# Linear attention and two expanding layers: weights converted in 512-column pieces in their own places, and 124 due times set one by one

## The chip, the cores and the metric

The kernel runs on one core of a Trainium2 chip. The metric is the device time of one execution in microseconds (us); a run's time is the median of its executions. Five engines work side by side, each on its own list of instructions in order: TensorE (PE in the rows; its weight loads are PEld), VectorE (DVE), ScalarE (ACT), GpSimd (POOL) and SyncE (SP), which here only issues transfers between the main memory and the on-chip memory.

## The reference

```python
def phi(x):                                   # x: q or k, [4, 8, 576, 64]
    proj = np.einsum('bhsd,df->bhsf', x, w_phi)            # 64 -> 128 features
    proj = proj - np.max(np.abs(proj), axis=-1, keepdims=True)
    return np.concatenate([np.exp(proj), np.exp(-proj)], axis=-1)
kv = einsum('bhsf,bhsd->bhfd', phi(k), v);  z = phi(k).sum(2)
x  = einsum('bhsf,bhfd->bhsd', phi(q), kv) / (einsum('bhsf,bhf->bhs', phi(q), z) + 1e-06)
x  = x.transpose(0, 2, 1, 3).reshape(2304, 512)
h = x @ w_in1;  x = where(h > 0, h, exp(min(h, 0)) - 1) @ w_out1     # 512 -> 2048 -> 512
h = x @ w_in2;  x = (h * cos(h)) @ w_out2                           # 512 -> 2048 -> 512
```

q, k, v and w_phi are float32. [...]

## The kernel before, in words

**Attention.** For each of the four batches, `keys` takes five tiles of 128 rows (the last has 64). Each tile is loaded (k, and v beside it), projected on PE in two halves, each half gets its largest magnitude and the difference on DVE (`shifted`), two exponentials on ACT, and a product with v on PE (`times_v`). For batch 0 the sums over the rows are a PE product with ones in the same step (L458); for the others DVE adds the exponentials up (L480). `sums` then copies and transposes the result. `queries` and `results` do the same for 18 tiles of q: projection, difference, transposes, exponentials, product (L571), reciprocal, result into `xy`.

**The two layers.** `block` goes over columns of `xy` (the token rows), `step` over 16 groups j of 128 hidden units. A step has a first product (`g1`, L710), the nonlinearity on ACT and DVE, and a second product (`g2`, L718). Each factor is split into a rounded high and a low part, and each product is three passes. Layer 1 runs in two parts: j = 0 to 7 in nine blocks of 256 columns, laid among the attention, then j = 8 to 15 in six of 384 columns. Then layer 2 in six blocks of 384 columns.

**The weights.** `convert` makes a high and a low float32 part of each float64 piece of 256 columns: the load from SP into one of four buffers `raw` (L350), two scalings on ACT (L353, L356), a shift and a joining on DVE (L360, L364), an addition on POOL (L368), the high part on ACT (L379), the low part on POOL (L382). A load waits until its `raw` buffer has been read, so the four buffers also hold the loads back.

**What sets the order.** Every piece of work is a task with an engine, an estimated duration and a due time. `plan` takes the tasks in time order on its own estimates: among those that can begin, the one with the earliest due time, in the place (a buffer or a bank) that comes free first. It counts 0.7 for the SP part of a weight load and a fixed delay until it has landed; how many bytes are under way it doesn't count. The order it finds is then written out on each engine, and there every engine works strictly in that order. Where the plan sees PE idle in the first 70 us, `keep_busy` puts matmuls of no use (`spare`, L826) in.

**Transfers.** All loads but the first two small ones are issued on SP, in one queue. In the program's order each transfer waits for the eighth before it to have landed (the semaphores DMAHW0 to DMAHW7 in the rows of order below), beside the wait for its place.

Of the kernel before, what the change touches and what calls it, by code (L numbers as in the profile page):

```python
# [8 lines left out]
F32 = mybir.dt.float32  # L9
# [20 lines left out]
CH = 256  # L30
NC = NK * P // CH
# [39 lines left out]
NL, W1LATE, NEQ, EARLY = 4, -24.05, 4, 176.41  # L71
# [4 lines left out]
ND, NKF, NVT, NQF, RAWB, NE = 5, 2, 2, 2, 4, 5  # L76
# [15 lines left out]
class Task:  # L92


    def __init__(self, engine, cost, due, fn, writes=(), reads=(), after=(), latency=None, port=False):
# [9 lines left out]
        self.bufs = [b for b in dict.fromkeys(list(writes) + list(reads)) if isinstance(b, Buf)]  # L105
# [114 lines left out]
def body(tc, qt, kt, vt, wphi, w1, w2, out):  # L220
# [81 lines left out]
    AP, AK, AQ = ("a0", "a1"), ("a2", "a3"), ("a0", "a1", "a2", "a3")  # L302

# [18 lines left out]
    LOWS = [("wa", f"l{i}") for i in range(2 * NC * JA + NL)]  # L322

    def columns(b, k):

        at = k * P % CH
        return b.tile[:, at:at + P]

    def convert(pool, m, j, due, pace=1.0, after=()):

        for io in range(2):
            for c in range(NC):
                h = [(pool, f"h{j}_{io}_{c}")]
                l = LOWS if pool == "wa" else [(pool, f"l{j}_{io}_{c}")]
                whole = Buf(LOWS, [P, CH])  # L340
                W[m, j, io, c] = Buf(h, [P, CH], F32R), Buf(l, [P, CH], F32R)
                convert_piece(whole, Buf(h, [P, CH], I32), m, j, io, c, due, after)
                split(whole, m, j, io, c, due)
                due += pace

    def convert_piece(f, r, m, j, io, c, due, after):
        raw = buf("stg", "raw", RAWB, [P, CH, 2], U32)

        def load():
            nc.sync.dma_start(raw.tile, ws[m][j, :, io, c * CH:(c + 1) * CH])  # L350

        def scale():
            nc.scalar.activation(f.tile, raw.tile[:, :, 1].bitcast(F32), AF.Copy, scale=2.0 ** -112)  # L353

        def rest():
            nc.scalar.activation(r.tile, raw.tile[:, :, 0], AF.Copy, scale=2.0 ** -29)  # L356

        def shift():
            e = f.tile.bitcast(U32)
            nc.vector.tensor_scalar(e, e, 3, None, ALU.logical_shift_left)  # L360

        def join():
            e = f.tile.bitcast(U32)
            nc.vector.scalar_tensor_tensor(e, raw.tile[:, :, 1], 0x80000000, e, ALU.bitwise_and, ALU.bitwise_or)  # L364

        def add():
            e = f.tile.bitcast(I32)
            nc.gpsimd.tensor_tensor(e, e, r.tile, ALU.add)  # L368

        task("SP", 0.7, due - 20, load, [raw], [f, r], after, latency=2.2)  # L370
        task("ACT", cost(ACT_, CH), due, scale, [f], [raw])
        task("ACT", cost(ACT_, CH), due, rest, [r], [raw])
        task("DVE", cost(DVE1, CH), due, shift, [f], port=True)
        task("DVE", cost(DVE_, CH), due, join, [f], [raw], port=True)
        task("POOL", cost(POOL_, CH), due, add, [f], [r])

    def split(f, m, j, io, c, due):
        h, l = W[m, j, io, c]
        task("ACT", cost(ACT_, CH), due, lambda: nc.scalar.copy(h.tile, f.tile), [h], [f])  # L379
# [43 lines left out]
    def keys(b, due, pace, after=()):  # L423
# [4 lines left out]
        for t in range(5):  # L428
            r, du = ST[t], due + t * pace
            kf, v = buf("at", "kf", NKF, [P, 4, P]), buf("at", "vt", NVT, [P, H, D])  # L430
            ds = [buf("at", "d", ND, [P, 4, NF]) for _ in range(2)]

            def load(kf=kf, t=t, r=r):
                nc.sync.dma_start(kf.tile[:, :, 0:r], kt[b, :, :, t * P:t * P + r])
# [4 lines left out]
            task("SP", 0.85, du - (20 if b else KLOAD), load, [kf], [], after, latency=2.2)  # L439
# [85 lines left out]
    def queries(T, due, pace):  # L525

        q = buf("at", "qf", NQF, [P, 4, P])
# [164 lines left out]
    def step(m, j, i, last, xs, xb, ys, yp, hs, N, due, pace, late):  # L692
        wi, wo = ([b for c in range(NC) for b in W[m, j, io, c]] for io in range(2))
# [30 lines left out]
        in_line("g1", task("PE", 12 * mr_cost(N), d1, g1, [hp], [*wi, *xb], line["g1"]))  # L724
# [46 lines left out]
        task("PE", 12 * mr_cost(N), d2, g2, ys, [sh, *wo])  # L771
# [118 lines left out]
```

## Time and profile before

| what | value |
|---|---|
| median of 3 runs | 997.42 us (996.88 to 998.33) |
| the profiled execution | 997.03 us |
| its span, first to last instruction | 995.2 us |
| PE busy | 982.6 us, 99% |
| DVE, ACT, POOL busy | 716.5, 504.3, 209.6 us |
| moved by transfers | 63.28 MB |

PE is busy for 99% of the span, but some of that is `spare` matmuls of no use, and all of the waiting is in the first tenth and behind the last product. So a change can only pay in the first 100 us, and it can lose anywhere. The stretch is to be read by engine and by the transfers, not by the averages over the span.

### The profile page before, as it was taken

The numbers are of one execution on the slowest core, as the hardware profiler recorded it, in microseconds if no ns is written. First come the engines' busy times: TensorE is split into PE (matmuls) and PEld (weight loads), VectorE is DVE, ScalarE is ACT, GpSimd is POOL, SyncE is SP. The second block draws the span as 40 slices with busy tenths as digits, with TensorE's granted clock in tenths as the row PEclk, the third lists the DMA queues.
The fourth block names the chain that finished last, engine by engine and source line by source line (L and its number), as shares of the span: only waits on it lengthen the run. The fifth ranks groups of instructions, "written<-read, shape, count | busy, mean of one in ns | idle before, by whom it ended". The sixth has DMA issues, their size and how long they took to land.

```text
span 995.2 us, 21100 instructions
## 1 busy us (share of the span) xinstructions
PE 982.6 (99%) x8422; PEld 944.5 (95%) x8422; DVE 716.5 (72%) x1423; ACT 504.3 (51%) x1196; POOL 209.6 (21%) x262
## 2 busy tenths in 40 slices
PE   8998999999999999999999999999999999999998
PEld 6787988988899999999999999999999999999998
DVE  6999978778676678988344679975666666756664
ACT  6886754545546768876322576742232332423322
POOL 3556300000002546674000265600000000000000
PEclk9999999999999999999999999999999999999999
DMA  7544212120103344442012232100000000000000
GB/s 235 174 125 141 87 49 81 34 69 19 46 12 97 96 127 144 154 149 75 1 33 74 75 106 77 63 33 1 1 33 1 1 33 1 32 1 1 32 1 32
DMA packets 45889, 63.28 MB, mean 64 GB/s; under 512 B 5728, under 2 KB 24800, under 8 KB 45792
## 3 DMA queue, kind: packets, MB, share of 16 engines
q1 hardware_dynamic: 45632, 61.88, 19.6%
q8 instruction: 66, 1.08, 0.5%
q14 instruction: 31, 0.25, 0.1%
q10 hardware_dynamic: 160, 0.07, 0.0%
HBM read 52.49 MB, written 9.44 MB: 62 GB/s over the span
## 4 chain that ended last, share of the span: by engine, by line
PE 90%; DVE 4%; ACT 2%; issue 1%; POOL 1%; DMA 1%; DVEq 0%
PE y L718 24%; PE h L710 23%; PE a L710 15%; PE a L718 15%; PE a L571 4%; PE a L399 3%; PE a L451 3%; PE a L548 1%; POOL l L368 1%; DVE m L412 1%; DVE l L364 1%; DVE ek L480 1%; DVE d L415 1%; DVE l L360 1%; PE y L458 1%
## 5 line engine op out<-in xcount | busy, mean ns | idle before, releaser
L710 PE MATMUL h<-x,h 128*128 128x256 f32 (+1 forms) x1152 | 253.0, 309 | 0.1
L718 PE MATMUL y<-s,h 128*128 128x256 f32 (+1 forms) x956 | 202.7, 304 | 0.4 <-DVE s L767 0.4
L710 PEld LDWEIGHTS h<-x,h 128*128 128x128 f32 x1152 | 191.6, 188 | 5.1 <-issue 3.3
L710 PE MATMUL h<-x,l 128*128 128x256 f32 (+1 forms) x576 | 176.6, 307 | 1.4 <-POOL l L382 1.4
L368 POOL TENSOR_TENSOR l<-l,h 128x256 int32<-128x256 int32 x128 | 105.9, 834 | 301.7 <-DMA raw<-w 189.8
L718 PEld LDWEIGHTS y<-s,h 128*128 128x128 f32 x956 | 156.2, 188 | 4.0 <-issue 1.9
L710 PE MATMUL a<-x,h 128*128 128x384 f32 x576 | 146.1, 334 | 0.0
L718 PE MATMUL y<-s,l 128*128 128x256 f32 (+1 forms) x478 | 143.8, 301 | 0.0
L382 POOL TENSOR_TENSOR l<-l,h 128x256 fp32r<-128x256 f32 x128 | 105.4, 832 | 132.2 <-ACT h L379 131.2
L710 PEld LDWEIGHTS h<-x,l 128*128 128x128 f32 x576 | 108.2, 188 | 1.6 <-POOL l L382 1.6
L752 ACT ACTIVATE gq<-gq,pihalf 128x384 f32<-128x384 f32 x96 | 59.2, 617 | 97.9 <-DVE gq L749 97.8
L710 PEld LDWEIGHTS a<-x,h 128*128 128x128 f32 x576 | 103.9, 188 | 0.0
L718 PE MATMUL a<-s,h 128*128 128x384 f32 x380 | 96.4, 334 | 0.0
L710 PE MATMUL a<-x,l 128*128 128x384 f32 x288 | 96.2, 334 | 0.0
L718 PEld LDWEIGHTS y<-s,l 128*128 128x128 f32 x478 | 89.8, 188 | 0.0
L379 ACT CAST h<-l 128x256 fp32r<-128x256 f32 x128 | 51.7, 406 | 42.6 <-POOL l L368 41.7
L364 DVE SCALAR_TENSOR_TENSOR l<-raw,l 128x256 uint32<-128x256 uint32 x128 | 68.7, 550 | 1.1
L718 PEld LDWEIGHTS a<-s,h 128*128 128x128 f32 x380 | 68.6, 188 | 0.0
L718 PE MATMUL a<-s,l 128*128 128x384 f32 x190 | 63.5, 334 | 0.0
L353 ACT ACTIVATE l<-raw 128x256 f32<-128x256 f32 x128 | 55.9, 437 | 10.1 <-DMA raw<-w 10.0
L767 DVE TENSOR_TENSOR s<-gq,s 128x384 fp32r<-128x384 f32 x95 | 58.6, 616 | 3.2 <-ACT s L263 0.8
L360 DVE TENSOR_SCALAR l<-l 128x256 uint32<-128x256 uint32 x128 | 51.3, 416 | 11.5 <-ACT l L353 9.5
(111 smaller groups left out, 1667.5 us busy)
## 6 DMA issues: line engine op xcount, KB each, us to landing
raw<-w SPq DMA_DIRECT2D x128, 256.0 KB, 3.0
qf<-qt SPq DMA_DIRECT2D x18, 256.0 KB, 2.7
part<-o SPq DMA_DIRECT2D x18, 256.0 KB, 2.4
oq<-part SPq DMA_DIRECT2D x12, 384.0 KB, 3.4
out<-oq SPq DMA_DIRECT2D x12, 384.0 KB, 2.5
kf<-kt SPq DMA_DIRECT2D x16, 256.0 KB, 3.5
vt<-vt SPq DMA_DIRECT2D x16, 256.0 KB, 2.9
kf<-kt SPq DMA_DIRECT2D x4, 128.0 KB, 3.5
```

The costliest lines, as they stand in the source:

```text
L353: nc.scalar.activation(f.tile, raw.tile[:, :, 1].bitcast(F32), AF.Copy, scale=2.0 ** -112)
L360: nc.vector.tensor_scalar(e, e, 3, None, ALU.logical_shift_left)
L364: nc.vector.scalar_tensor_tensor(e, raw.tile[:, :, 1], 0x80000000, e, ALU.bitwise_and, ALU.bitwise_or)
L368: nc.gpsimd.tensor_tensor(e, e, r.tile, ALU.add)
L379: task("ACT", cost(ACT_, CH), due, lambda: nc.scalar.copy(h.tile, f.tile), [h], [f])
L382: nc.gpsimd.tensor_sub(l.tile, f.tile, h.tile.bitcast(F32))
L399: nc.tensor.matmul(pp[odd].tile[0:r, i * NF:(i + 1) * NF], x.tile[rows, i, 0:r], ww[rows], start=(i == 0), stop=True, skip_group_check=True,)
L571: nc.tensor.matmul(ns[odd].tile[32 * h:32 * h + 32, g * P + lo:g * P + hi], k[:, half, h // 2, at:at + 32] if g < 2 else k[:, half, 2, 32 ...
L710: nc.tensor.matmul(hp.tile[:, 0:N], columns(W[m, j, 0, kk * P // CH][a], kk), xs[kk][c](), start=(kk == 0 and n == 0), stop=(kk == NK - 1 ...
L718: nc.tensor.matmul(yp(dt), columns(W[m, j, 1, dt * P // CH][a], dt), (hi, lo)[c](), start=(i == 0 and n == 0 and (late or dt % 2 == 0)), s ...
L752: nc.scalar.activation(g.tile[:, 0:N], g.tile[:, 0:N], AF.Sin, bias=pihalf)
L767: nc.vector.tensor_sub(lo(), g.tile[:, 0:N], hi().bitcast(F32))
```

## The change

A weight piece is now 512 columns (half as many instructions, each twice as wide). Its raw numbers land where the high and low part will lie in the end, so that no `raw` buffers are left and a load of layer 1 waits for no buffer. The work in between is in three buffers `f` of two halves. Key and query tiles share four places `xf` in place of two `kf` and two `qf`. The key tile 2 of batch 0 is loaded from ACT's queue. The first four query tiles may use the banks h0, h1 and y0 too. And `MOVED` sets the due time of 124 tasks, by their number, and for some the engine.

```diff
-ND, NKF, NVT, NQF, RAWB, NE = 5, 2, 2, 2, 4, 5
+ND, NXF, NVT, NE = 5, 4, 2, 5
+NF_, RLEAD = 3, 20.0
+TEX, ONACT = 4, 3
+MOVED = {
+    2: -47, 10: 623, 14: 538, 26: 86, 36: 242, 46: 65, 52: -99, 53: -27, 54: -0, 58: -35, 66: 122, 68: -96,
...
+        moved = MOVED.get(len(tasks), t.due)
+        t.due, only = moved if isinstance(moved, tuple) else (moved, None)
+        t.choice = {only: t.choice[only]} if only else t.choice
...
+    AE = (*AQ, "h0", "h1", "y0")
...
-        raw = buf("stg", "raw", RAWB, [P, CH, 2], U32)
+    def convert_piece(place, m, j, io, due, after):
+        raw, w = Buf(place, [P, WD, 2], U32), Buf(place, [P, 2 * WD], F32R)
+        f = buf("stg", "f", NF_, [P, 2, WD])
+        W[m, j, io] = w
...
-            nc.sync.dma_start(raw.tile, ws[m][j, :, io, c * CH:(c + 1) * CH])
+            nc.sync.dma_start(raw.tile, ws[m][j, :, io])
...
-        task("SP", 0.7, due - 20, load, [raw], [f, r], after, latency=2.2)
+        task("SP", 0.7, due - RLEAD, load, [raw], [], after, latency=3.4)
...
+        task("ACT", cost(ACT_, WD), due, high, [w], [f])
+        task("POOL", cost(POOL_, WD), due, low, [w], [f])
...
-            kf, v = buf("at", "kf", NKF, [P, 4, P]), buf("at", "vt", NVT, [P, H, D])
+            kf, v = buf("at", "xf", NXF, [P, 4, P]), buf("at", "vt", NVT, [P, H, D])
...
+            side = b == 0 and 2 <= t < ONACT
+            queue = nc.scalar if side else nc.sync
...
-        shifted(q, due, P, ds, () if T < QFREE else done, (*AQ, "h0", "h1") if T < 2 else AQ)
+        shifted(q, due, P, ds, () if T < QFREE else done, (*AQ, "h0", "h1") if T < 2 else AQ if T >= TEX else AE)
...
+        ax = AE if T < TEX else AQ
+        tts, ns = [bank(*ax) for _ in range(2)], [bank(*ax) for _ in range(2)]
```

On SP, the loads that stand around the v tile of key tile 2 in batch 0 (vt0_58) in the kernel before; raw is a weight piece, kf a key tile, qf a query tile, and the brackets hold what each waits for:

```order
L350 DMA raw0_48_258<-w1 128x512 [waits DMAHW6_49,DVE_49,Activation_49]
L350 DMA raw1_53_268<-w1 128x512 [waits DMAHW7_49,DVE_49,Activation_49]
L434 DMA kf0_57_293<-kt 128x4x64 [waits DMAHW2_49,DMAHW0_49,PE_49]
L437 DMA vt0_58_302<-vt 128x512 [waits DMAHW1_49,PE_49]
L350 DMA raw2_66_324<-w1 128x512 [waits DVE_49,Activation_49]
L350 DMA raw3_70_333<-w1 128x512 [waits DMAHW3_49,DVE_49,Activation_49]
L437 DMA vt1_78_353<-vt 128x512 [waits DMAHW4_49,PE_49]
```

The same place now (vt0_50 is that v tile, w2_0 the first half of the weights of j = 2, xf2_45 a query tile):

```order
L364 DMA w2_0_31_203<-w1 128x1024 [waits DMAHW6_49]
L364 DMA w2_1_34_210<-w1 128x1024 [waits DMAHW7_49]
L364 DMA w3_0_39_234<-w1 128x1024 [waits DMAHW0_49]
L364 DMA w4_1_41_240<-w1 128x1024 [waits DMAHW1_49]
L364 DMA w5_0_44_247<-w1 128x1024 [waits DMAHW2_49]
L546 DMA xf2_45_252<-qt 128x512 [waits DMAHW3_49,PE_49]
L364 DMA w5_1_48_275<-w1 128x1024 [waits DMAHW4_49]
L364 DMA w6_0_49_280<-w1 128x1024 [waits DMAHW5_49]
L453 DMA vt0_50_283<-vt 128x512 [waits DMAHW6_49,PE_49]
L364 DMA w6_1_57_303<-w1 128x1024 [waits DMAHW7_49]
L364 DMA w7_0_58_307<-w1 128x1024 [waits DMAHW0_49]
L364 DMA w7_1_64_325<-w1 128x1024 [waits DMAHW1_49]
```

Of weights, six pieces of 256 columns stand ahead of that v tile on SP before, and eleven of 512 columns now; they no longer wait for DVE and ACT. In all, 18 weight pieces of 512 columns stand ahead of the v tile of key tile 4 (vt0_89).

On PE, the end of batch 0's keys and the first transposes of a query tile (L548) before, with vt0_98 the v tile of key tile 4:

```order
L399 MATMUL a_107_461<-ww,qf_33_188 128x128
L451 MATMUL a_40_225<-ek_95_414,vt_98_439 64x256 x4
L451 MATMUL a_41_226<-ek_97_436,vt_98_439 64x256 x4
L458 MATMUL y_42_227<-ek_95_414,ones 32x256 x4
L458 MATMUL y_42_227<-ek_97_436,ones 32x256 x4
L548 MATMUL a_123_521<-ident,d_93_402 128x128 x4
L548 MATMUL a_124_522<-ident,d_94_403 128x128 x4
```

And now:

```order
L412 MATMUL a_92_432<-ww,xf_71_358 128x128
L565 MATMUL h_95_444<-ident,d_78_374 128x128 x4
L565 MATMUL h_96_445<-ident,d_79_375 128x128 x4
L467 MATMUL a_35_212<-ek_82_390,vt_89_420 64x256 x4
L467 MATMUL a_36_213<-ek_87_416,vt_89_420 64x256 x4
L474 MATMUL y_37_214<-ek_82_390,ones 32x256 x4
L474 MATMUL y_37_214<-ek_87_416,ones 32x256 x4
```

The transposes went ahead of the last product with v, into the banks h0 and h1. The rest of batch 0's keys stands on PE as before. Of `spare` matmuls there are 25 in place of 35, 10 in place of 12 of them ahead of key tile 2.

On POOL, the additions and low parts of weights for j = 9 to 12 before (l3, l26, l28 are places of the work in between):

```order
L368 TENSOR_TENSOR l28_901_4966<-l28_901_4966,h9_1_1_902_4967 128x256
L382 TENSOR_TENSOR l9_1_1_920_5079<-l28_901_4966,h9_1_1_919_5075 128x256
L368 TENSOR_TENSOR l3_909_5005<-l3_909_5005,h10_0_0_910_5006 128x256
L368 TENSOR_TENSOR l26_913_5014<-l26_913_5014,h10_0_1_914_5015 128x256
L382 TENSOR_TENSOR l10_0_0_926_5118<-l3_909_5005,h10_0_0_923_5100 128x256
L382 TENSOR_TENSOR l10_0_1_931_5128<-l26_913_5014,h10_0_1_927_5120 128x256
```

And now, the same stage:

```order
L382 TENSOR_TENSOR f0_826_5067<-f0_826_5067 128x512
L388 TENSOR_TENSOR w10_1_829_5104<-f0_826_5067,w10_1_829_5104 128x512
L382 TENSOR_TENSOR f0_834_5140<-f0_834_5140 128x512
L388 TENSOR_TENSOR w12_1_846_5221<-f0_834_5140,w12_1_846_5221 128x512
L382 TENSOR_TENSOR f0_849_5243<-f0_849_5243 128x512
L388 TENSOR_TENSOR w13_1_854_5295<-f0_849_5243,w13_1_854_5295 128x512
```

Nine pieces in a row go through f0 alone there: f1 and f2 hold pieces whose low part stands far behind in the order.

## Rows read from the trace of the kernel before

**Rows 1.** The page's part 1: busy us, share of the span, instructions by engine.
```profile
PE 982.6 (99%) x8422; PEld 944.5 (95%) x8422; DVE 716.5 (72%) x1423; ACT 504.3 (51%) x1196; POOL 209.6 (21%) x262
```

**Rows 2.** Windows: stretch, length, busy PE, PEld, DVE, ACT, POOL, PE clock, transfer share, GB/s.
```profile
0.00:3.00 3.00, 1.64 (x7) 1.64 (x8) 0.13 (x3) 1.03 (x1) 0.70 (x6) 1.00 0.14 36
3.00:12.00 9.00, 7.79 (x59) 7.23 (x57) 5.28 (x11) 3.93 (x10) 0.00 (x0) 1.00 1.01 313
8.00:10.00 2.00, 2.00 (x12) 1.78 (x11) 2.00 (x5) 1.43 (x5) 0.00 (x0) 1.00 1.06 389
12.00:25.00 13.00, 13.00 (x162) 8.30 (x160) 10.39 (x22) 11.70 (x29) 7.66 (x10) 1.00 0.72 225
40.00:100.00 60.00, 56.33 (x790) 47.60 (x788) 58.95 (x117) 46.24 (x120) 38.13 (x40) 1.00 0.44 135
100.00:200.00 100.00, 99.73 (x1463) 90.27 (x1466) 82.27 (x164) 55.62 (x132) 9.41 (x13) 1.00 0.21 62
200.00:372.00 172.00, 170.54 (x2187) 160.58 (x2176) 121.84 (x257) 98.65 (x252) 30.41 (x39) 1.00 0.22 65
372.00:900.00 528.00, 527.56 (x3098) 527.36 (x3097) 368.38 (x716) 246.41 (x574) 115.25 (x144) 1.00 0.16 52
```

**Rows 3.** The chain that ended last, first 130 us: start us, us, what.
```profile
8.54 3.58 PE spare L826 x24
...
21.19 1.88 PE a L451 x16
...
24.07 1.09 PE h L399 x16
...
31.00 1.00 PE y L458 x16
...
33.12 1.57 ACT eq L557 x3
...
63.61 0.29 issue
...
100.58 0.87 PE a L548 x8
101.45 0.66 PE a L517 x6
102.11 1.41 PE y L718 x12
...
126.38 2.76 PE a L571 x96
```

**Rows 4.** Issues of the v tiles in the first 12 us, and their landing.
```profile
L437 SPq DMA_DIRECT2D vt<-vt x2: 430/431/432, 2.9 to 4.4; - x2
...
DMA to landing us min/median/max: 5.4/5.7/6.0
```

**Rows 5.** DVE's timeline at the copy of batch 0's sums.
```profile
35.52 0.41 DVE L265 COPY ks<-y 128x256 f32<-128x256 f32 x1
```

**Rows 6.** DVE's groups, 35 to 102 us: busy us, mean ns of one, idle before.
```profile
L412 DVE TENSOR_REDUCE m<-a 128x4 f32<-128x512 f32 x14 | 9.0, 679 | 0.0
...
L364 DVE SCALAR_TENSOR_TENSOR l<-raw,l 128x256 uint32<-128x256 uint32 x22 | 8.7, 413 | 0.0
L480 DVE TENSOR_TENSOR ek<-ek,ek 128x1024 f32<-128x1024 f32 x6 | 8.7, 1475 | 0.0
L360 DVE TENSOR_SCALAR l<-l 128x256 uint32<-128x256 uint32 x22 | 8.0, 392 | 0.1
L587 DVE RECIPROCAL rd<-rd 128x128 f32<-128x128 f32 x8 | 7.0, 914 | 0.0
L767 DVE TENSOR_TENSOR s<-g,s 128x256 fp32r<-128x256 f32 x7 | 3.4, 489 | 0.0
```

**Rows 7.** POOL's groups, 300 to 372 us, columns as in the group before.
```profile
L368 POOL TENSOR_TENSOR l<-l,h 128x256 int32<-128x256 int32 x20 | 15.8, 795 | 209.4 <-DMA raw<-w 189.8 <-DVE l L364 15.6 <-ACT g L731 2.4
L382 POOL TENSOR_TENSOR l<-l,h 128x256 fp32r<-128x256 f32 x19 | 15.0, 794 | 9.8 <-ACT h L379 9.8
```

More of the change, by code (lines that the diff above doesn't have):

```diff
@@ L321, in body, with columns @@
     W = {}
-    LOWS = [("wa", f"l{i}") for i in range(2 * NC * JA + NL)]
-    def columns(b, k):
-        at = k * P % CH
+    def columns(b, part, k):
+        at = part * WD + k * P
         return b.tile[:, at:at + P]
@@ L336, in convert @@
         for io in range(2):
[L337 to L346, printed above, removed]
-        raw = buf("stg", "raw", RAWB, [P, CH, 2], U32)
+            convert_piece([(pool, f"w{j}_{io}")], m, j, io, due, after)
@@ L366, in add @@
+            nc.vector.scalar_tensor_tensor(e, word(1), 0x80000000, e, ALU.bitwise_and, ALU.bitwise_or)
         def add():
             e = f.tile.bitcast(I32)
-            nc.gpsimd.tensor_tensor(e, e, r.tile, ALU.add)
-        task("SP", 0.7, due - 20, load, [raw], [f, r], after, latency=2.2)
[L371 to L379, printed above, removed]
-        def low():
-            nc.gpsimd.tensor_sub(l.tile, f.tile, h.tile.bitcast(F32))
-        task("POOL", cost(POOL_, CH), due, low, [l], [f, h])
+            nc.gpsimd.tensor_tensor(e[:, 0], e[:, 0], e[:, 1], ALU.add)
+        def high():
+            nc.scalar.copy(w.tile[:, 0:WD], f.tile[:, 0])
@@ new lines, in low @@
+        def low():
+            nc.gpsimd.tensor_sub(w.tile[:, WD:], f.tile[:, 0], w.tile[:, 0:WD].bitcast(F32))
+        task("SP", 0.7, due - RLEAD, load, [raw], [], after, latency=3.4)
+        task("ACT", cost(ACT_, WD), due, scale, [f], [raw])
+        r = task("ACT", cost(ACT_, WD), due, rest, [], [raw], uses=[f])
+        task("DVE", cost(DVE1, WD), due, shift, [f], port=True)
+        task("DVE", cost(DVE_, WD), due, join, [f], [raw], port=True)
+        task("POOL", cost(POOL_, WD), due, add, [f], [], [r])
@@ L429, in keys, with load @@
             r, du = ST[t], due + t * pace
-            kf, v = buf("at", "kf", NKF, [P, 4, P]), buf("at", "vt", NVT, [P, H, D])
+            kf, v = buf("at", "xf", NXF, [P, 4, P]), buf("at", "vt", NVT, [P, H, D])
             ds = [buf("at", "d", ND, [P, 4, NF]) for _ in range(2)]
-            def load(kf=kf, t=t, r=r):
-                nc.sync.dma_start(kf.tile[:, :, 0:r], kt[b, :, :, t * P:t * P + r])
+            side = b == 0 and 2 <= t < ONACT
+            queue = nc.scalar if side else nc.sync
+            def load(kf=kf, t=t, r=r, queue=queue):
+                queue.dma_start(kf.tile[:, :, 0:r], kt[b, :, :, t * P:t * P + r])
             def load_v(v=v, t=t, r=r):
                 nc.sync.dma_start(v.tile[0:r], vt[b, t * P:t * P + r])
-            task("SP", 0.85, du - (20 if b else KLOAD), load, [kf], [], after, latency=2.2)
+            task("ACT" if side else "SP", 0.6 if side else 0.85, du - (20 if b else KLOAD), load, [kf], [], after, latency=2.2)
             task("SP", 0.85, du - (15 if b else VLOAD), load_v, [v], [], after, latency=2.2)
@@ L692, in step @@
     def step(m, j, i, last, xs, xb, ys, yp, hs, N, due, pace, late):
-        wi, wo = ([b for c in range(NC) for b in W[m, j, io, c]] for io in range(2))
+        wi, wo = W[m, j, 0], W[m, j, 1]
         hp = bank(*hs)
@@ L710, in g1 @@
                     nc.tensor.matmul(
-                        hp.tile[:, 0:N], columns(W[m, j, 0, kk * P // CH][a], kk), xs[kk][c](),
+                        hp.tile[:, 0:N], columns(wi, a, kk), xs[kk][c](),
                         start=(kk == 0 and n == 0), stop=(kk == NK - 1 and n == 2),
```

36 lines of the change are left out of this document (21 added, 15 removed), and 7 rows, old and new, of the table MOVED.

## The prediction

> **What bounds the kernel now.** I read the page's engine shares first, then windows by stage, then the chain of waits of the first 130 us, and last the transfers. The page gives PE 982.6 of 995.2 us [rows 1], which says little alone, since `spare` matmuls count as busy. The windows say where it can be changed [rows 2]: from 100 to 900 us PE is busy for 99.73 of 100, 170.54 of 172 and 527.56 of 528 us. All that a better order could win there is 2.2 us. In 40 to 100 us it is DVE that is full, 58.95 of 60, and PE works on what DVE hands over. Before that PE itself sets the pace: in 12 to 25 us it is busy for all 13 us, with batch 0's keys, in the chain a product with v of 1.88, ones of 1.00 and a projection of 1.09 for each tile [rows 3]. The transfers are the third: from 3 to 12 us their share is 1.01 at 313 GB/s, so they were full, and from then on 0.72 [rows 2].
>
> So three quantities tell the time: when PE ends batch 0's keys (32.00 us, the end of the row at 31.00 [rows 3]), how long DVE then takes to the last product that PE waits for, and how much PE work lies before that product. What PE has lost there is in the end time, since PE is full from then on.
>
> **The transfers, first part.** This is where the change costs. Before, the loads of weights were held back by four buffers that DVE and ACT had to read first; now the raw numbers go to their own places and only the wait for the eighth transfer before is left. The v tile of key tile 2 stands behind eleven weight pieces of 128 x 1024 x 4 bytes, 0.524 MB each, 5.77 MB; with the other key, query and v tiles, itself included (nine full ones of 0.262 MB and a half one), and the small weights 8.32 MB. For key tile 3 it is 14 pieces and 10.16 MB, for tile 4 it is 18 and 12.91 MB. With eight transfers under way the queue doesn't run empty, so a tile lands when the bytes ahead of it are through.
>
> Until 12 us the rows moved 3 x 36 + 9 x 313 GB/s = 2.92 MB [rows 2], and the changed order has as much to move in that time. That the queue serves in order is seen in the second v tile: it is the seventh on SP, 1.90 MB with its own and the small weights, and these are through at 3 + 1.79/0.313 = 8.7 us. It was issued at 4.4, and the two v tiles landed 5.4 and 6.0 after their issue [rows 4]; with the longer time it landed at 10.4, 1.7 behind the bytes.
>
> For the rate behind 12 us there is 313 GB/s as the mean of the full stretch and 389 as the best two microseconds of it [rows 2]. The rows have no transfer with 4 KB in a partition, as the new weight loads have; I take 370, in the upper half between the two, since wider pieces should not be slower, and keep both ends. Then tile 2's v lands at 12 + 5.40/0.370 + 1.7 = 28.3 us, tile 3's at 12 + 7.24/0.370 + 1.7 = 33.3, tile 4's at 12 + 9.99/0.370 + 1.7 = 40.7.
>
> PE wants them much earlier. Tile 2's product began at 21.19 [rows 3]; with four passes of `spare` less ahead (of 24 in 3.58 us, 0.15 each) it would begin at 20.6. The query projection and all that follows stand behind it on PE. So: wait to 28.3, product and ones 2.88, projection 1.09, at 32.3; wait to 33.3, product and ones, projection, transposes of 0.87 (now put here), at 38.1; wait to 40.7, product and ones, done at 43.6. Before it was 32.00: 11.6 later, with one step of 0.9 more behind it, a loss of 10.7. That ACT's queue brings key tile 2 early, the four shared places, the extra banks and the ten `spare` matmuls fewer are worth nothing more here: what they save is spent waiting for v.
>
> **DVE, second part.** The copy of the sums begins 0.2 after the ones and takes 0.41 [rows 5], so DVE goes on at 44.2. Then it has, up to the difference that the transposes at the end of batch 1's keys need: 14 maxima, 14 differences, 7 shifts and 7 joins of 512 columns, 6 reciprocals, 6 results, 6 `elu`, 4 low parts of s and 4 of x, 8 additions of exponentials, 5 copies. By the durations of [rows 6]: 9.5 + 9.5 + 5.5 + 2.5 + 2.5 + 2.0 + 2.0 + 11.8 + 2.1 = 47.4 (a difference as a maximum, both of 512 columns; results, `elu` and copies as a join of 256), and the weights. A join of 512 is 0.413 plus the 0.27 by which a maximum of 512 columns is longer, 0.69; a shift 0.392 plus half of that, 0.53. Seven of each are 8.5 (fourteen of 256 were 11.3). In all 55.9. The groups of that window add up to 72 us in 67, as starts overlap ends, so 0.93 of it: 52.0 us, to 96.2, and 0.2 to PE, 96.4.
>
> PE's work between is 7 projections, 2 transposes, 3 attention products of 2.76, 5 products with v, 10 half steps of 1.41, 1.0 for sums and 18 small turns of 0.11 [rows 3]: 44.2. So it loses 96.4 - 43.6 - 44.2 = 8.6 there. Before, from 32.00 to the product at 102.11, which comes behind 57.1 of the same kinds of work (8, 5, 4, 5, 14, 1.0 and 24), it lost 13.0. The new order is better by 4.4 in this stretch: it has transposes and a projection ahead, and less DVE work for each us of PE work.
>
> **Sum.** 10.7 - 4.4 = +6.3 us on the profiled execution's 997.03: 1003.3. The execution lies 0.4 below the median of 997.42, so it stands for it. At 389 GB/s tile 4's v lands at 39.4 and the keys end at 42.3: +5.0, 1002.0. At 313 it lands at 45.6, they end at 48.5: +11.2, 1008.2.
>
> The Trainium skill, "DMA: Bandwidth & Descriptors", section "Bandwidth", says that large transfers come closer to the peak, and measures 425 GB/s for 16 MB against 341 for 1 MB. By its 425 the keys would end at 40.1 us, and the sum be +2.8, 999.8, an estimate. The rows' best two microseconds stay below it, so I don't take it.
>
> **Behind 100 us.** ACT saves three of six instructions for 512 columns and SP half of its issues: nothing, since PE is full there. The conversions of the second half of layer 1 go through one place f0 for nine pieces, in 21 steps of 2.81 us (two half steps), 59 us or 6.6 for each piece. A piece takes two POOL operations one behind the other, each 1.6 (twice 0.795 [rows 7]), on ACT two in line of 0.52 each (a third of 1.57 [rows 3]), on DVE 0.53 and 0.69, and seven handovers at up to 0.29, as one in the chain [rows 3]: 5.5 without these, 7.5 with all at the most. So it fits, or is late by up to 0.9. From below it could give back the 1.5 us that PE lacks in 200 to 372 us, from above it costs 9 x 0.9 = 8.1, if ACT and DVE are kept from the steps behind. I take nothing, as 6.6 is in the middle.
>
> **Rivals.**
> First, that the weights don't hold v up (the queue is faster, or small loads pass large ones). Then PE ends the keys at 32.3 with the extra step done, DVE ends at 84.9, and PE has lost 0.6 less in the first stretch and 4.4 less in the second: -5.0, 992.0. This is the other side, faster. It decides from a landing of tile 2's v at 20.6, for which 5.40 MB would have to pass in 6.9 us, 780 GB/s: against it is every row, for it only that a queue of this length does not occur in the trace.
> Second, the loss is paid back: the queue runs at 389, and DVE has 4 us less to do, because additions of exponentials (1475 ns where POOL is at work) and shifts (392) find POOL at rest. 1002.0 - 4 = 998.0, no change. For it: 512 columns at once leave POOL longer pauses; against it: POOL's work is as much as before.
> Third, the one place f0: the delayed start stays and the steps in 310 to 372 us stretch by half of the 8.1: 1007.3. For it is the bare fit; against it, that PE has a step's work ahead in its banks.
>
> **Chances.** The forecast 0.46 (its own range 999 to 1008), no hold-up 0.17, paid back 0.19, f0 0.18. A difference of 0.2%, 2 us, is about what can be told from none. Slower: 0.42 of the forecast and f0's 0.18, 0.60. The same: paid back and a part of the forecast, 0.20. Faster: no hold-up and the edge of paid back, 0.20. The range goes from 993 to 1009: it leaves out most of the first rival and the far end of the third.
>
> **What would show it.** In the changed profile the transfer share should stay at 1 from 3 to about 41 us, with v tiles landing some 10 us after their issue, and PE should wait for v at the product of key tile 2 (some 8 us), 3 and 4. Batch 0's last ones should end near 44 us in place of 32, and DVE should be full from there to 96. Wrong would be a v of tile 2 that lands before 23 us, or PE waiting for something else in the first 45 us. The third rival would show as PE waits between 310 and 372 us, at products behind DVE or ACT.

## The result and the profile after

The changed kernel takes 1006.85 us, the median of 6 runs from 1003.36 to 1008.10; the kernel before took 997.39 beside it (6 runs, 996.88 to 999.69). The ratio of the means is 1.0083, 95% interval 1.0061 to 1.0105 (ratios below are of means too). The execution with the profile took 1003.36 us, its span is 1001.6. It is one of the two fastest of the six; what the other four have in addition is a question of its own, below.

The page's part 1 of the changed kernel, to be held against [rows 1]:

```profile
PE 982.8 (98%) x8402; PEld 943.4 (94%) x8402; DVE 681.1 (68%) x1277; ACT 492.8 (49%) x1022; POOL 174.4 (17%) x134
```

DVE has 35 us less to do, POOL 35, ACT 12, and the kernel is slower all the same: busy time summed over the span doesn't tell what lies on the path. The windows say where the time went (columns as in [rows 2]):

```profile
3.00:12.00 9.00, 8.05 (x60) 7.35 (x60) 5.50 (x10) 3.34 (x6) 0.00 (x0) 1.00 1.00 322
12.00:25.00 13.00, 8.80 (x112) 5.51 (x109) 11.14 (x18) 11.43 (x22) 7.16 (x6) 0.95 1.02 357
25.00:30.00 5.00, 1.26 (x6) 0.85 (x8) 0.55 (x1) 2.54 (x5) 1.08 (x1) 0.50 1.03 411
30.00:35.00 5.00, 5.00 (x42) 2.50 (x40) 0.00 (x0) 0.70 (x2) 0.00 (x0) 0.60 1.05 383
35.00:40.00 5.00, 5.00 (x61) 3.36 (x60) 3.77 (x7) 2.82 (x6) 1.34 (x2) 1.00 0.98 321
40.00:50.00 10.00, 8.92 (x92) 6.73 (x91) 8.41 (x17) 8.79 (x17) 6.79 (x5) 1.00 0.33 93
100.00:200.00 100.00, 98.73 (x1489) 89.45 (x1491) 83.06 (x151) 58.37 (x137) 12.98 (x10) 1.00 0.21 63
200.00:300.00 100.00, 100.00 (x1500) 90.55 (x1492) 74.77 (x138) 50.75 (x116) 0.00 (x0) 1.00 0.13 36
300.00:372.00 72.00, 71.95 (x753) 71.19 (x742) 50.15 (x104) 48.72 (x115) 25.47 (x20) 1.00 0.37 133
```

The transfers are full from 3 to 40 us; before, their share fell to 0.72 from 12 us on [rows 2]. In 25 to 35 us DVE and ACT hardly work, and TensorE's granted clock is 0.50, 1.2 GHz, from 25 to 30 us, in its idle stretch and behind it. From 100 to 372 us PE lacks 1.3 us, where it lacked 1.7 before [rows 2]. PE's timeline (start us, us, line, what, and in brackets the wait before it) names what it waited for:

```profile
28.74 3.68 PE L467 MATMUL a<-ek,vt 128*64 128x256 f32 x16 [7.94 <-DMA vt<-vt]
...
35.25 1.95 PE L467 MATMUL a<-ek,vt 128*64 128x256 f32 x16
...
41.07 1.94 PE L467 MATMUL a<-ek,vt 64*64 64x256 f32 x16 [0.76 <-DMA vt<-vt]
42.95 1.07 PE L474 MATMUL y<-ek,ones 64*32 64x256 f32 x16
```

Tile 2's product waits 7.94 us for its v and then runs at half clock, 3.68 us in place of 1.95. Batch 0's last ones end at 42.95 + 1.07 = 44.02 us; in the kernel before this was 32.00 [rows 3]. The chain of the first 130 us has three transfers in it that are not in the one of before:

```profile
14.31 8.71 DMA w<-w
23.04 9.43 DMA w<-w
32.53 8.41 DMA vt<-vt
...
97.18 0.87 PE h L565 x8
```

and the v tiles of 14 to 45 us (DMA's issues, then the time from issue to landing) took up to 10.1 us. In the kernel before the tiles of the same stretch had taken 4.0 at the most; its lines stand second (the 5.4 and 6.0 of [rows 4] are the two tiles ahead of these):

```profile
L453 SPq DMA_DIRECT2D vt<-vt x5: 328/333/512, 18.5 to 43.0; - x5
...
DMA to landing us min/median/max: 2.5/8.4/10.1
```

```profile
L437 SPq DMA_DIRECT2D vt<-vt x5: 327/328/513, 15.2 to 31.0; - x5
...
DMA to landing us min/median/max: 2.5/3.4/4.0
```

Of the changed kernel's five, batch 0's tiles 2, 3 and 4 took 10.1, 8.4 and 8.4 us.

Two numbers for each execution make all that follows readable: when batch 0's last ones end, and the span less that, here called the rest. Before: 32.00 and 995.2 - 32.00 = 963.2. After: 44.02 and 957.6. So the first part lost 12.0 us, and the rest won 5.6.

### The profile page after: what moved, and what is told of

It is laid out like the page before. It is cut to its first block, busy times and chain, and to the rows that moved or that the text cites. A ratio compares the mean times of both kernels' runs of the same rounds, so it can differ in the third digit from the quotient of the medians.

```text
span 1001.6 us, 20361 instructions
## 1 busy us (share of the span) xinstructions
PE 982.8 (98%) x8402; PEld 943.4 (94%) x8402; DVE 681.1 (68%) x1277; ACT 492.8 (49%) x1022; POOL 174.4 (17%) x134
## 4 chain that ended last, share of the span: by engine, by line
PE 86%; DMA 5%; DVE 3%; issue 2%; ACT 2%; POOL 2%; SPq 0%; POOLq 0%; ACTq 0%; DVEq 0%
PE y L735 23%; PE h L727 23%; PE a L735 14%; PE a L727 14%; PE a L588 4%; DMA w<-w 3%; PE a L412 3%; PE a L467 3%; PE a L565 1%; POOL f L382 1%; DMA vt<-vt 1%; POOL w L388 1%; DVE m L425 1%; DVE ek L496 1%; PE a L533 1%
## 5 line engine op out<-in xcount | busy, mean ns | idle before, releaser
L727 PE MATMUL h<-x,w 128*128 128x256 f32 (+1 forms) x1728 | 273.3, 308 | 0.3 <-DVE gq L772 0.3
L727 PEld LDWEIGHTS h<-x,w 128*128 128x128 f32 x1728 | 255.6, 188 | 3.8 <-issue 1.6
L735 PE MATMUL y<-s,w 128*128 128x256 f32 (+1 forms) x1428 | 225.5, 303 | 0.5 <-DVE s L784 0.5
L735 PEld LDWEIGHTS y<-s,w 128*128 128x128 f32 x1428 | 204.0, 188 | 4.7 <-issue 2.9
L727 PE MATMUL a<-x,w 128*128 128x384 f32 x864 | 159.4, 334 | 0.0
L382 POOL TENSOR_TENSOR f<-f 128x512 int32<-128x512 int32 x64 | 88.7, 1391 | 355.3 <-ACT f L367 185.8
L727 PEld LDWEIGHTS a<-x,w 128*128 128x128 f32 x864 | 150.6, 188 | 0.0
L735 PE MATMUL a<-s,w 128*128 128x384 f32 x564 | 113.0, 334 | 0.0
L388 POOL TENSOR_TENSOR w<-f,w 128x512 fp32r<-128x512 f32 x64 | 85.7, 1345 | 105.3 <-ACT w L385 105.3
L735 PEld LDWEIGHTS a<-s,w 128*128 128x128 f32 x564 | 99.1, 188 | 0.2 <-DVE s L784 0.2
```

The source lines that it names most:

```text
L382: nc.gpsimd.tensor_tensor(e[:, 0], e[:, 0], e[:, 1], ALU.add)
L388: nc.gpsimd.tensor_sub(w.tile[:, WD:], f.tile[:, 0], w.tile[:, 0:WD].bitcast(F32))
L727: nc.tensor.matmul(hp.tile[:, 0:N], columns(wi, a, kk), xs[kk][c](), start=(kk == 0 and n == 0), stop=(kk == NK - 1 and n == 2),)
L735: nc.tensor.matmul(yp(dt), columns(wo, a, dt), (hi, lo)[c](), start=(i == 0 and n == 0 and (late or dt % 2 == 0)), stop=(last and n == 2), ...
```

## The experiments

Theory: the weight pieces, no longer held back by four buffers, stand ahead of v in SP's queue, and v is late by their length. Rivals: the new order of DVE's and POOL's work costs the time; TensorE's half clock costs it. Where an edit reads `vload[b, t]`, the tile of v and its load task are kept there when the task is made. Of each edit the lines that matter are shown; `order` is the plan's list of tasks. In every one but the sixth, the ninth and the twelfth only SP's order, a queue, or `spare` products differ from the changed kernel.

**1. v ahead of pieces.**

```diff
-        for t in plan(tasks, dict.fromkeys(pools, 0.0)):
+        order = plan(tasks, dict.fromkeys(pools, 0.0))
+        pieces = [t for t in order if t.fn.__name__ == "load" and t.engine == "SP" and t.bufs[0].places[0][0] == "wa"]
+        for k, n in ((2, 7), (3, 7), (4, 11)):
+            load = vload[0, k][1]
+            order.remove(load)
+            order.insert(order.index(pieces[n]), load)
+        for t in order:
```

> Edit: the changed kernel with SP's order alone edited: the loads of batch 0's v tiles 2 and 3 stand ahead of the eighth weight piece, that of v tile 4 ahead of the twelfth; every other engine's order is the changed kernel's. Theory (the backlog of weight pieces in the queue holds v back): v tile 2 lands at 20 to 22 us in place of 28.7, batch 0's keys end near 35 us or before in place of 44.0, and the time comes down by most of 10.7 us of hold-up less the 4.4 us that DVE's second part gave back: 992 to 997 us. Rival 1 (the new order of DVE's and POOL's work costs the time, v's lateness is hidden): 1003 to 1008 us as before. Rival 2 (TensorE's fall to half clock costs it): the clock stays at 2.4 GHz here too, so only the amount tells, 1000 or less.

Measured: 1007.70 us (4 runs, 1002.47 to 1009.03), 1.0097 of before (1.0069 to 1.0124). A miss. PE's timeline:

```profile
23.29 3.43 PE L467 MATMUL a<-ek,vt 128*64 128x256 f32 x16 [2.60 <-DMA vt<-vt]
...
36.06 1.83 PE L412 MATMUL a<-ww,xf 64*128 64x128 f32 x16 [4.38 <-DMA xf<-qt]
...
41.70 1.07 PE L474 MATMUL y<-ek,ones 64*32 64x256 f32 x16
```

v comes 5.4 us earlier, but the wait goes to a query tile, whose projection stands ahead of tile 4's product on PE: its load now stood behind v tile 4, which waited for its place, and three pieces. The ones end at 42.77, the rest is 957.9. So the time says nothing against the theory yet: the backlog was moved, not taken away.

**2. v on the other queue.**

```diff
-                nc.sync.dma_start(v.tile[0:r], vt[b, t * P:t * P + r])
+                own = nc.scalar if b == 0 and t >= 2 else nc.sync
+                own.dma_start(v.tile[0:r], vt[b, t * P:t * P + r])
```

> Edit: the changed kernel with batch 0's v tiles 2, 3 and 4 issued on ACT's DMA queue in place of SP's, at the same places of the program. Theory, if a transfer of the second queue passes the pieces that stand in the first: v tile 2 lands 3 to 5 us after an issue near 19 us, in place of 10, and the time is 994 to 999 us. If the transfer engines serve both queues in order of issue, or share them so that v gets half: landing 6 to 10 us behind the issue, 1000 to 1007 us. Rival 1 (order of DVE and POOL): 1003 to 1008 us whenever v lands.

Measured: 1007.33 us (4 runs, 1001.50 to 1008.35), 1.0091 (1.0061 to 1.0120). DMA's issues of v and their landing, then PE's timeline:

```profile
L454 ACTq DMA_DIRECT2D vt<-vt x3: 334/353/502, 16.2 to 26.8; - x3
...
DMA to landing us min/median/max: 6.5/6.8/7.1
```

```profile
23.46 1.95 PE L468 MATMUL a<-ek,vt 128*64 128x256 f32 x16 [2.41 <-DMA vt<-vt]
...
36.12 2.17 PE L412 MATMUL a<-ww,xf 64*128 64x128 f32 x16 [4.45 <-DMA xf<-qt]
...
43.73 1.93 PE L475 MATMUL y<-ek,ones 64*32 64x256 f32 x16
```

On a queue with nothing else in it by then, v lands 6.5 to 7.1 us behind its issue, less than the 8.4 to 10.1 of the same tiles in the first queue and more than the 2.5 to 4.0 of the kernel before: it passes pieces, but it isn't free of them. The Trainium skill, "DMA: Bandwidth & Descriptors", section "Queues, rings and completion order", says that each transfer engine takes turns between the queues that have work for it; these landings agree. The end is set by the same query tile as in the first experiment, in SP's queue, and tile 4's ones, at half clock behind that wait, end at 45.66.

**3. The wait filled.**

```diff
             def times_v(es=es, v=v, t=t, r=r):
+                if b == 0 and t == 2:
+                    for _ in range(46):
+                        nc.tensor.matmul(spare[:, 0:P], ident, ident, start=True, stop=True)
```

> Edit: the changed kernel with 46 spare 128x128 products on TensorE ahead of key tile 2's product, some 7.7 us of work in the 7.9 us that it waits for v there. Theory (hold-up by transfers): the clock stays up, tile 2's product and ones take 1.95 and 1.07 us in place of 3.68 and 1.87, but v tile 4 still lands at 41 us and sets the end of batch 0's keys: 1003 to 1004 us in every execution, with less spread than 1003.4 to 1008.1 if the slower executions came from the clock. Rival 2 (the clock's fall is what costs): 1000 us or less. Rival 3 (the spread is from the transfers): 1003 to 1008 us, spread as before.

Measured: 1003.87 us (4 runs, 1003.48 to 1006.54), 1.0074 (1.0059 to 1.0089). The mean granted clock of the runs is 1.000, 0.999 and 1.000 at 1003.48, 1003.48 and 1004.25 us, and 0.996 at 1006.54, the one with the trace:

```profile
21.14 10.54 PE L466 MATMUL spare<-ident 128*128 128x128 f32 x92
...
42.05 1.94 PE L470 MATMUL a<-ek,vt 64*64 64x256 f32 x16 [1.40 <-DMA vt<-vt]
43.92 1.91 PE L477 MATMUL y<-ek,ones 64*32 64x256 f32 x16
```

With the clock up throughout, three of four runs stay where the fastest of the changed kernel are: the half clock does not cost what the profiled execution lost. In the fourth the clock fell all the same, behind the wait of 1.40 us for v tile 4: the ones take 1.91 us. v tile 4 still sets the end, as the theory has it. (The 46 products took 10.54 us, more than meant, and that is hidden too.)

**4. A smaller backlog.**

```diff
+        for t in [t for t in order if t.engine == "SP" and t.bufs and t.bufs[0].places[0][0] == "wc"][:2]:
+            order.remove(t)
+            order.insert(order.index(vload[1, 2][1]), t)
```

> Edit: the changed kernel with the two pieces of step 8, 1.05 MB that nothing reads before 60 us, moved in SP's order from behind its first five loads and from its 29th place to behind the first keys of batch 1; nothing else moves. Theory (hold-up): at 370 GB/s v tile 2 lands 1.4 us earlier (one of the two stood ahead of it) and v tile 4 2.8 us earlier or 1.4 us where it is its wait for the other that counts: 1000.5 to 1002.5 us against 1003.4. Rival 1 (order of DVE and POOL): no change, 1003.4 to 1008.

Measured: 1002.75 us (4 runs, 1001.07 to 1003.35), 1.0059 (1.0042 to 1.0075).

```profile
27.90 3.68 PE L467 MATMUL a<-ek,vt 128*64 128x256 f32 x16 [6.62 <-DMA vt<-vt]
...
40.98 1.07 PE L474 MATMUL y<-ek,ones 64*32 64x256 f32 x16
```

Against the changed kernel's trace the wait is 1.3 us shorter, the ones end 1.97 earlier, the span is 2.3 shorter. The first dose that goes as the theory says.

**5. No piece before its time.** The rule that the first experiment lacked: every piece waits, so that nothing that is wanted early stands behind one.

```diff
+        for load in [t for t in order if t.fn.__name__ == "load" and t.bufs[0].places[0][0] in ("wa", "wc") and t.start < 40]:
+            want = min(t.start for t in load.next) - 20
+            if want > load.start:
+                order.remove(load)
+                at = next(t for t in order if t.engine == "SP" and t.start >= want)
+                order.insert(order.index(at), load)
```

> Edit: the changed kernel, with every early weight piece's load moved back in SP's order to 20 us before its first reader by the plan's own times (v tiles 2 and 3 then stand behind 6 pieces in place of 11 and 14, tile 4 behind 9 in place of 18, and no query or key load stands behind a piece that nothing reads before 45 us). Every other engine's order is unchanged. Theory (hold-up by the backlog, which the first experiment only moved from v to a query tile): no data of batch 0 is late, v tile 2 lands at 20 to 22 us, batch 0's keys end at 32 to 34 us, TensorE's clock stays at 2.4 GHz, and the time is the 992.0 us of the prediction's case without a hold-up, 990 to 994. Rival (the new order of DVE's and POOL's work is worth nothing or costs, so that DVE's second part ends as late as in the kernel before): 997 to 999 us with batch 0's keys ending near 32 us all the same, TensorE waiting later in the first 100 us.

Measured: 995.33 us (9 runs, 993.67 to 1000.29), 0.9989 (0.9975 to 1.0002): some 11 us from the changed kernel by SP's order alone, 9.3 of them in the end of the ones of the two traces and a part of the others in the clock.

```profile
22.83 1.95 PE L467 MATMUL a<-ek,vt 128*64 128x256 f32 x16 [1.53 <-ACT w L385]
...
33.67 1.07 PE L474 MATMUL y<-ek,ones 64*32 64x256 f32 x16
```

The ones end at 34.74, and the rest is 993.5 - 34.74 = 958.8. The name in the bracket is misleading: the tile's last exponential had ended at 21.0, and v, issued at 15.35, landed 7.3 us later, at 22.7; it was v again, 1.5 us late. The theory holds; that wait is 1.5 of the 3.3 us by which its 992.0 was missed.

**6. A backlog for the kernel before.** Six transfers of 0.52 MB from main memory to main memory (NDUM is 6, `spill` a place there) that nobody reads, ahead of one load.

```diff
                 def load_v(v=v, t=t, r=r):
+                if b == 0 and t == 2:
+                    for n in range(NDUM):
+                        nc.sync.dma_start(spill[n], ws[2][NJ - 1 - n // 2, :, n % 2])
                 nc.sync.dma_start(v.tile[0:r], vt[b, t * P:t * P + r])
```

> Edit: the kernel before with 6 transfers of 0.524 MB from device memory to a scratch in device memory, that nothing reads, issued on SP's queue just ahead of the v tile of key tile 2; the rest is the kernel before, word for word. Theory (a backlog in the queue costs its length): v tile 2 lands some 8.5 us late (3.15 MB at 370 GB/s), batch 0's keys end at 38 to 40 us in place of 32.0, and the time is 1003 to 1006 us, or some 3 us more where TensorE's clock falls in the wait. Rival (paid back: TensorE waits 13.0 us for DVE between 35 and 100 us, and DVE works on while v is late): 997 to 999 us.

Measured: 1006.42 us (4 runs, 1005.98 to 1007.69), 1.0098 (1.0084 to 1.0112).

```profile
28.75 3.51 PE L456 MATMUL a<-ek,vt 128*64 128x256 f32 x16 [7.46 <-DMA vt<-vt]
...
40.13 1.07 PE L463 MATMUL y<-ek,ones 64*32 64x256 f32 x16
```

The ones end 9.2 us later than before, 41.20, the rest is 1004.5 - 41.20 = 963.3, as before to 0.1. So a late v costs its whole length in the old order too, with the old order's DVE work: nothing is paid back, and a backlog alone makes a loss of this size. With the fifth, where the new order stands without the backlog and loses nothing, the first rival (the new order of DVE's and POOL's work) is out. 1.56 of the 9.2 is tile 2's product at half clock.

**7. The changed kernel again.**

> No edit: the changed kernel again, to see the spread of its executions (1003.4 to 1008.1 us) beside a trace. Theory (TensorE's clock): executions of 1006 us and more have a lower mean granted clock than those near 1003.4 (0.993 against 0.994 so far); if a profile shows one of them, its stretch from 25 to 60 us has more time at 1.2 GHz, batch 0's keys end some 3 to 4 us behind 44.0, and from there to the end it takes the same 957.6 us. Rival (transfers): such an execution has its v tiles landing 3 to 4 us later at an unchanged clock.

Measured: 1007.27, 1008.71 and 1004.48 us at mean clocks of 0.993, 0.991 and 0.995; 1.0097 (1.0082 to 1.0112). The trace is of the first. A window, then PE's timeline:

```profile
40.00:50.00 10.00, 8.27 (x57) 5.43 (x58) 3.71 (x9) 5.54 (x11) 3.22 (x3) 0.66 0.23 67
```

```profile
41.73 2.35 PE L467 MATMUL a<-ek,vt 64*64 64x256 f32 x16 [2.27 <-DMA vt<-vt]
44.01 1.93 PE L474 MATMUL y<-ek,ones 64*32 64x256 f32 x16
```

Tile 4's v lands 0.7 us later than in the first trace, and the wait for it is 2.27 in place of 0.76 us; behind it the clock falls a second time, 0.66 in 40 to 50 us in place of 1.00, and the ones, turns and projections take up to twice as long. The ones end at 45.94, 1.9 later, and the rest is 959.6, 2.0 longer: 3.9 in all, between the groups of 1003.4 and 1007 to 1008. The theory's size is right; of its details the end of the keys carries only half, the other half is half-speed work just behind it. And 0.7 of the 3.9 is the later landing, the rival's part.

**8. One piece and one query tile less ahead of v tile 2,** in the fifth kernel.

```diff
+        v2 = vload[0, 2][1]
+        order.remove(v2)
+        pieces = [t for t in order if t.fn.__name__ == "load" and t.bufs[0].places[0][0] == "wa"]
+        order.insert(order.index(pieces[5]), v2)
```

> Edit: the kernel of the fifth experiment with the load of v tile 2 moved one piece and one query tile further ahead in SP's order (it then stands behind 5 pieces in place of 6). In the fifth experiment that tile landed at 22.7 us, 7.3 us behind its issue, and TensorE waited 1.5 us for it. Theory (hold-up): 0.79 MB less ahead of it at 350 GB/s is 2.2 us, the wait of 1.5 us goes, batch 0's keys end at 33.2 in place of 34.7 us, and the time is 993.5 to 994 us with no execution at a lower clock. Rival (the piece or the query tile that lands later becomes the wait, or ACT does): 995 to 996 us as before.

Measured: 998.16 us (12 runs, 992.70 to 1000.11), 0.9997 (0.9982 to 1.0012), in two groups: five runs at 992.7 to 995.7 us with a mean clock of 0.998 to 1.000, seven at 998.0 to 1000.1 with 0.994 to 0.997. The trace is of the first group:

```profile
21.14 1.95 PE L467 MATMUL a<-ek,vt 128*64 128x256 f32 x16
...
32.03 1.07 PE L474 MATMUL y<-ek,ones 64*32 64x256 f32 x16
```

The wait is gone, the ones end at 33.10 as expected and the rest is 957.8: 992.7, the prediction's first rival to 0.7. But more than half of the runs lose it, and these have the lower clock; none of them has a trace.

**9. Without the extra banks,** in the fifth kernel.

```diff
-TEX, ONACT = 4, 3
+TEX, ONACT = 0, 3
```

> Edit: the kernel of the fifth experiment without the extra banks for the transposes and products of the first four query tiles (TEX = 0), which re-plans the order of the first 100 us; pieces, shared places and due times stay. It asks where the 4.4 to 5.9 us come from by which the changed order does the stretch behind batch 0's keys faster than the kernel before. Theory (less DVE work by pieces of 512 columns, and transposes ahead): most of it stays, 995 to 997 us. Rival (the banks give it): all of it goes, 998.5 to 1001 us.

Measured: 1103.19 us, 1.1065 (1.1049 to 1.1081). PE's waits behind 372 us:

```profile
PE a L727 <- ACT w L385: 45.6, 1, 45.6
PE h L727 <- ACT w L385: 34.7, 1, 34.7
```

Of the 106 us that it is slower, 80 are in these two waits at the conversions of layer 1's second half, far from the banks. Why the conversions come so late there was not looked into; that the due times set one by one fit only the plan that they were set for is a guess. The time tells nothing about the banks.

**10. The short wait filled.** The fifth experiment, with the third one's edit and `range(6)`.

> Edit: the kernel of the fifth experiment with 6 spare 128x128 products on TensorE ahead of key tile 2's product (46 took 10.54 us in the third experiment, so 6 take 1.4), in the 1.5 us that it waits for v there. Two of nine executions of the fifth experiment had a mean granted clock of 0.996 and took 997.0 and 1000.3 us, the other seven 0.999 to 1.0 and 993.7 to 995.7. Theory (the clock falls in some executions behind that wait): all executions at 0.999 to 1.0, 993.5 to 996 us, median near 995. Rival (the clock falls elsewhere): some executions at 0.994 to 0.997 and 997 to 1000 us as before.

Measured: 994.45 us (6 runs, 993.90 to 995.53, all at 0.999 or 1.000), 0.9970 (0.9959 to 0.9982): faster than both kernels.

```profile
22.77 1.95 PE L470 MATMUL a<-ek,vt 128*64 128x256 f32 x16 [0.32 <-DMA vt<-vt]
...
33.61 1.07 PE L477 MATMUL y<-ek,ones 64*32 64x256 f32 x16
```

The rest is 992.5 - 34.68 = 957.8.

**11. The eighth again,** beside the tenth on the same chip.

> No edit: the kernel of the eighth experiment again, whose executions fell in two groups (992.7 to 995.7 us at a mean clock of 0.998 to 1.0, and 998.0 to 1000.1 at 0.994 to 0.997), to see one of the second group in a trace. Theory (clock): such a trace has a stretch at 1.2 GHz in the first 60 us, behind an idle stretch of TensorE, and the same time from the end of batch 0's keys to the end. Rival: the clock falls behind 100 us, in the blocks, where TensorE never waits. If the trace is again of the first group it says nothing.

Measured: 994.73 us (9 runs, 992.70 to 996.41; seven at 0.999 or 1.000, two at 0.998), 0.9969 (0.9960 to 0.9979). The trace is of the slowest, at 0.998. PE's timeline, then a window:

```profile
31.50 1.95 PE L467 MATMUL a<-ek,vt 64*64 64x256 f32 x16 [1.04 <-DMA vt<-vt]
33.37 1.35 PE L474 MATMUL y<-ek,ones 64*32 64x256 f32 x16
```

```profile
35.00:40.00 5.00, 4.82 (x38) 4.18 (x36) 3.31 (x6) 3.44 (x7) 2.35 (x2) 0.76 0.31 112
```

Here too it is a v tile that comes a little late, a wait of 1.04 us, and a fall of the clock behind it, in the first 60 us and not in the blocks. The same kernel gave 0.9997 on another chip, where seven of twelve runs had the lower clock. So whether the six products of the tenth experiment keep the clock up is not shown: without them, on its chip, seven of nine runs were clean.

**12. Halves.** The tenth kernel, with DVE's two steps of a piece issued as two of 256 columns each.

```diff
-            e = f.tile[:, 0].bitcast(U32)
-            nc.vector.tensor_scalar(e, e, 3, None, ALU.logical_shift_left)
+            for c in range(0, WD, 256):
+                e = f.tile[:, 0, c:c + 256].bitcast(U32)
+                nc.vector.tensor_scalar(e, e, 3, None, ALU.logical_shift_left)
...
+            for c in range(0, WD, 256):
+                e = f.tile[:, 0, c:c + 256].bitcast(U32)
+                nc.vector.scalar_tensor_tensor(e, word(1)[:, c:c + 256], 0x80000000, e, ALU.bitwise_and, ALU.bitwise_or)
```

> Edit: the kernel of the tenth experiment with DVE's shift and join of each weight piece issued as two of 256 columns in place of one of 512; no order changes. It asks what part of the 4.4 to 5.9 us of the stretch behind batch 0's keys the longer instructions give. In the kernel before a join of 256 took 0.413 us and a shift 0.392, so two of each are 1.61 us a piece; in the tenth experiment a join of 512 took 0.764 and a shift 0.600, 1.36 a piece; 11 or 12 pieces stand between 34 and 100 us: 2.8 us more of DVE's work. Theory (DVE bounds that stretch, and its lighter work is part of the gain): 2 to 3 us of the gain go, 996.5 to 997.5 us. Rival (the gain is the order alone, DVE has room): 994 to 995 us as before.

Measured: 1002.20 us (6 runs, 1001.09 to 1005.28), 1.0055 (1.0043 to 1.0067). DVE's groups of 34 to 100 us (count, busy us, mean ns of one), of the twelfth kernel and then of the tenth:

```profile
L375 DVE TENSOR_SCALAR f<-f 128x256 uint32<-128x256 uint32 x24 | 12.0, 547 | 0.0
...
L380 DVE SCALAR_TENSOR_TENSOR f<-w,f 128x256 uint32<-128x256 uint32 x24 | 8.7, 412 | 0.0
```

```profile
L378 DVE SCALAR_TENSOR_TENSOR f<-w,f 128x512 uint32<-128x512 uint32 x12 | 8.9, 764 | 0.0
...
L374 DVE TENSOR_SCALAR f<-f 128x512 uint32<-128x512 uint32 x11 | 6.4, 600 | 0.0
```

The ones end as in the tenth, at 34.82, and the rest grows by 7.5 us. Two runs at a mean clock of 1.000 took 1001.09 and 1001.84, so it is not the clock, though the traced execution, at 0.997, has a little of that too (0.83 from 40 to 50 us). A piece costs DVE 2 x 547 + 2 x 412 = 1918 ns in place of 600 + 764 = 1364; twelve of them are 6.6 us. So DVE bounds the stretch behind the keys nearly one for one. The size was missed because a shift of 256 took 547 ns here and 392 in the kernel before [rows 6]. These are means, and they mix two kinds of shifts, as the spread shows (count, then ns min/median/max; the twelfth kernel, then the tenth):

```profile
L375 DVE TENSOR_SCALAR f<-f x24: 273/282/1422, 33.8 to 99.5; 128x256 uint32<-128x256 uint32 x24
...
L374 DVE TENSOR_SCALAR f<-f x11: 408/417/1548, 35.4 to 95.3; 128x512 uint32<-128x512 uint32 x11
```

Most take about 280 or 415 ns. The long ones began while POOL was at work, and lasted until it was done; of the twelfth kernel, DVE's row and then POOL's:

```profile
53.38 1.42 DVE L375 TENSOR_SCALAR f<-f 128x256 uint32<-128x256 uint32 x1
...
53.37 1.28 POOL L390 TENSOR_TENSOR w<-f,w 128x512 fp32r<-128x512 f32 x1
```

The shift ends at 54.80 us, 0.15 behind POOL; so do the five others over 1 us. Halves make twice as many shifts that can meet POOL: seven of 24 began so here, three of eleven in the tenth. So the 7.5 us are not what the long pieces gain over the kernel before, whose shift and join of 256 took 392 and 413 ns, 1610 a piece [rows 6]: by that, twelve pieces gain 12 x (1610 - 1364) ns = 3.0 us, an estimate.

## Why the prediction was right

**What bounds the kernel** was read rightly: behind 100 us little moved. PE got back 1.4 us in 200 to 372 (100.00 and 71.95 of 172, where 170.54 had been [rows 2]) and lost 1.0 in 100 to 200 (98.73 for 99.73), so that to take nothing there came out right as a sum of the two.

**The transfers.** Forecast: v tile 2 usable at 28.3 us, tile 4 at 40.7, ones ending at 43.6. Measured: 28.74, 41.07, 44.02. The rate of 370 GB/s, chosen between 313 and 389, was 365 as the mean of 12 to 40 us (13 us at 357, 5 each at 411, 383 and 321). The Trainium skill's 425 for large transfers ("DMA: Bandwidth & Descriptors", section "Bandwidth") is not reached in any of these windows; the sum by it, 999.8, was 3.6 too low even for this execution. That the loss is caused by the backlog, and by no other part of the change, is shown from three sides: taken away by order alone the ones end 9.3 us earlier (fifth), a smaller one gives a part (fourth), and put into the kernel before it costs 9.2 us there (sixth). The step on tile 3 was wrong and harmless: its product waited for PE, since tile 2's ran at half clock.

**DVE, second part.** Forecast: transposes at 96.4 us, 4.4 us won there and 0.9 for the step put ahead, together 5.3 of the rest. Measured: 97.18, and a rest 5.6 shorter; without the backlog it is 4.4 to 5.4 shorter (fifth, eighth and tenth). That DVE's work bounds this stretch is shown by the twelfth, and by its estimate the longer pieces give some 3 us of the gain; what the banks and the order give of the others was not told apart, since the ninth failed.

**Sum.** +6.3 forecast, 1003.36 - 997.03 = +6.3 in the profiled execution, and 1006.85 - 997.39 = +9.5 by the medians. The agreement to a tenth is luck: the first part was 0.4 longer than forecast, the rest 0.3 shorter, and the profile fell on one of the two fastest executions.

**The rivals.** No hold-up: v would have had to pass at 780 GB/s; it did not, but the time worked out for this case, 992.0, is what the kernel reaches once the hold-up is taken away, 992.7 in the best runs. Paid back: the additions of exponentials did fall, to 1379 ns from the 1475 of [rows 6] (128x1024, six each; 44 to 97 us in the changed kernel), 0.6 us in all, but the sixth experiment shows that lateness as such is not paid back. The one place f0: PE is busy for 71.95 of 72 us from 300 to 372, so it did not occur.

**What was missing** is a term for TensorE's clock. The sum took the wait for v as idle time and no more. Behind it the granted clock was 0.50. In the profiled execution that is hidden, as tile 4's v comes later still; in the trace of the seventh experiment the clock fell again behind the wait for tile 4, and that made some 3.2 us of 3.9. The median of six, 1006.85, lies 3.5 above the sum; the one trace of such an execution puts most of that down to this term. The range held it.

## What to carry to other kernels

A buffer that seems only to hold loads back may be what keeps them out of the way: in a queue served in order, taking such a limit off puts bulk that is needed late ahead of small tiles that are needed now. Place each load by its first reader, and look at everything that then stands behind it, not only at the tile that was late. Split every execution at the end of the stage that the change touches: two numbers, the end and the rest, told most of the experiments apart where the times alone did not. A wait of an engine with a granted clock has a price beside its length, and it differs from run to run.

## What the runs showed of the hardware

- With transfers full, a v tile of 0.13 to 0.26 MB landed 8.4 to 10.1 us behind its issue in the queue of the weights and 6.5 to 7.1 in the other queue (second experiment); in the kernel before, where the transfer share was 0.72, 2.5 to 4.0. Not every transfer of the other queue was quick: the changed kernel's key tile 2, issued there at 2.0 us, landed 9.5 us later.
- TensorE's clock fell to 1.2 GHz behind idle stretches of 7.94, 2.27 (seventh), 1.40 (third) and in one execution 1.04 us (eleventh); in others, waits of 2.41 us (second) and 1.53 us (fifth) left it at 2.4 GHz. The same kernel had a lower mean clock in seven of twelve runs on one chip and, less deep, in two of nine on another.
- A shift on DVE took 282 ns at the median for 256 columns and 417 for 512. Of 20 that began while POOL was at work (34 to 100 us of the kernel before, the changed one, the tenth and the twelfth), 19 lasted until POOL was done, up to 1.56 us.
